# Attention and feed-forward mix on one core: float32 P·V steps in one piece of 512 columns, with a scheduler clock that counts instruction fetches

## The chip, the core and the metric

The kernel runs on one core of a Trainium2 chip. A core has a matrix engine (PE; its weight loads are listed as PEld), a vector engine (DVE), a scalar engine (ACT), a general engine (POOL) and a queue engine that here only starts transfers (SP). Each works through its own list of instructions in order and waits on semaphores for the others. Matmuls write PSUM banks, and the other engines read them from there. The metric is the device time of one execution in microseconds (us).

## The reference

`x` is 2048 x 512. The attention has 32 heads of width 16 with one shared key and value head (`wk`, `wv`: 512 x 16), and no mask; the feed-forward layer has width 1792.

```python
q = (x @ wq).reshape(B, S, H, Dh).transpose(0, 2, 1, 3)
k, v = x @ wk, x @ wv
p = softmax(einsum("bhqd,bkd->bhqk", q, k) * Dh ** -0.5)
a = einsum("bhqk,bkd->bhqd", p, v).transpose(0, 2, 1, 3).reshape(B, S, H * Dh) @ wo
b = einsum("bsf,fd->bsd", silu(einsum("bsd,df->bsf", x, w1)), w2)
g = sigmoid((x * gate_w).sum(-1, keepdims=True))
return g * a + (1 - g) * b
```

## The kernel before

**Stages.** A short first stage (to the first exponential) loads and transposes `x`, makes the keys `KT`, the values `VF` (float32) and `VP` (two halves of 16 columns in 16-bit form), the gate and the first queries. The long stage after it, `attention`, runs the attention and the feed-forward layer together. A second, slower pass over everything stands in the program behind a branch that this input does not take; its instructions are in the program and never run.

**Rounds, steps and scores.** Queries are worked in 32 rounds: 4 chunks of 512 rows x 4 groups of heads x 2 halves. A round has 16 steps, one for each block of 128 keys, so there are 512 steps. A step has two scores (1024 in all). A score (`scores`, L1165) is 8 matmuls of 32 x 512 that fill one of two buffers `S`; then ACT takes the exponential of 128 x 1024 values into half of `P` (L1171). Score number p + 2 reuses the buffer of score p, so it waits for the exponential of p.

**The sums P V** (`sums`, L1260) multiply the step's `P` (128 x 4 x 512) with the values into two accumulators `pv`. There are two ways to do a step:

- *float32* (units "a" and "b"): `P` as it is, with `VF`. Before the change each unit takes 256 of the 512 columns, 8 matmuls in the program, except at the first step of a round, which takes all 512 columns in one piece, again 8 matmuls. The hardware runs one such float32 matmul as two matmuls with two weight loads, so a piece costs 32 PE instructions whether it has 256 or 512 columns.
- *split* (units "U" and "L"): the upper 16 bits of `P` read in place as bfloat16, and the rest, `L`, which DVE makes as a float16 tile by one subtraction of 128 x 2048 (L1190). Each unit is 8 matmuls and 8 weight loads.

Which step goes which way is decided by the scheduler. Even steps are due to be split; an odd step may be split when DVE has time and no other `L` is held (the condition in `scores` with `SPARE`).

**Everything else on PE** is cut into slots of 4 or 8 matmuls: feed-forward layer, output projection and later queries (`Out.product`, L826; `f_slot`). A slot interleaves the tail of one product (rows 64 to 127) with the head of the next (rows 0 to 63). At the end, what remains is done with whole matmuls of 128 columns (`Out.whole`, L830). Products end on DVE (`acc`, L800) or, for the hidden layer, on ACT (tanh into `e`, L840), DVE (L845) and POOL (`H`, L847, L848).

**What sets the order.** The program is written out by a planner in Python. It keeps a clock for PE, ACT, DVE and POOL (`pe[0]`, `act[0]`, ...) with constant costs: a slot of PE takes `SLOT` = 0.2165 us, a U or L unit `VSLOT`, an `L` on DVE `LOW`. In the main loop it works out `due`, the time at which the next score may start (when the exponential two before it has ended), and `room`, the time left until `due + LATER`. It then chooses: sums that fit into `room`, a slot of other work, or the score. `HURRY`, `LASTB`, `NEAR` and `FRESH` say when sums go ahead of slots, and `PB` how many `P` tiles there are. Nothing of this clock is in the program that runs: it only fixes the order on each engine.

Of the kernel before, what the change touches and what calls it, by code (L numbers as in the profile page):

```python
# [25 lines left out]

SLOT, VSLOT, LOW, V_PART = 0.2165, 0.23, 2.37, 1.7
LATER, HURRY, PIECE, PB, FIRST_LOW, LASTB, NEAR, FRESH, SPARE = 0.2, 4, 5.6, 5, 6, 4, 6, 6, 2  # L30

FIRST = "EEEEEEEEEESEESEEEESEEEESBEEEE"
AHEAD, EARLY = 2, (4, 5)
# [14 lines left out]
def kernel(  # L48
# [39 lines left out]
    VF = consts.tile([128, NKT, 32], F32)  # L88
# [648 lines left out]
    def attention(ctx, scale_of, t_scale, shifts, split_pieces, chores, q_todo, bounds, early, gates_, later):  # L737
# [7 lines left out]
        pe, act, dve, pool = [0.0], [0.0], [0.0], [0.0]  # L745
        tasks, L = [], {}

        def put(dur, ready, due, f, hard=False, low=None):

            tasks.append([due, ready, dur, f, hard, low])  # L750
            return tasks[-1]
# [226 lines left out]
        class Turn:  # L978

            cur = new = None  # L980
            i = n = 0
# [59 lines left out]
        def f_slot():  # L1041
            i, cur, new = T_.i, T_.cur, T_.new
            for m in range(4):
                if new and i < new.n:
                    new.product(i, lo, m, i == 0, False)
                if cur and i >= T_.n - cur.n:
                    cur.product(i - T_.n + cur.n, hi_, m, False, i == T_.n - 1)
            pe[0] += SLOT
            if cur and i == T_.n - 1:
                leave(cur)  # L1050
            T_.i += 1
            if T_.i == T_.n:
                T_.cur, T_.new, T_.going, T_.since, T_.chain = new, None, False, scored[0], bool(cur)
# [28 lines left out]
        steps = [(i, kt) for i in range(len(rounds)) for kt in range(NKT)]  # L1082
# [67 lines left out]
        def scores(p):  # L1150
            s, j = divmod(p, 2)
            i, kt = steps[s]
            if p % 2 == 0 and kt == 0:
                prefetch(i + 1)
                if q_todo and i % 2 == 0:
                    queue.append(q_todo.pop(0))
            if j == 0:
                probs[s] = wp.tile([128, 4, 512], F32, name="P", bufs=PB)
            sc = pS.tile([128, 2, 512], F32, name="S")
            pe[0] = max(pe[0], ends.get(p - 2, 0.0) + 0.05)  # L1160
            for m in range(4):
                for f in range(2):
                    b = 64 * f
                    k0 = kt * 128 + 32 * m
                    nc.tensor.matmul(sc[32 * m:32 * m + 32, f], KT[b:b + 50, k0:k0 + 32], qtile[i][b:b + 50, j], start=True, stop=True)  # L1165
            begin = max(act[0], pe[0] + 0.48)
            pe[0] += SLOT
            scored[0] += 1
            P = probs[s]
            c, o, _ = rounds[i]  # L1170
            nc.scalar.activation(P[:, 2 * j:2 * j + 2], sc, AF.Exp, scale=scale_of(c, o))  # L1171
            act[0] = begin + 0.902
            ends[p] = begin + 1.018
            if j and s % 2 == 0:
                if s >= FIRST_LOW or not later:
                    lows[s] = put(LOW, ends[p] + 0.06, ends[p] + 2.66, lambda: low(s), low=lambda: len(L) < 2)
                else:
                    native.add(s)
            elif j and s >= FIRST_LOW:
                lows[s] = put(LOW, ends[p] + 0.06, ends[p] + 40, lambda: low(s), low=lambda: not L and s >= first[0] + SPARE)  # L1180
# [13 lines left out]
        native, units, opened, first, v_end = set(), {}, set(), [0], [1e9 if later else 0.0]  # L1194

        def units_of(s):

            if s in units:
                return units[s]
            return ["U", "L"] if s in low_end or s % 2 == 0 and s not in native else ["a", "b"]  # L1200
# [4 lines left out]
        def can_go(s):  # L1205
            i = steps[s][0]
            if not units_of(s) or ends.get(2 * s + 1, 1e9) + 0.05 > pe[0]:
                return False
            if i and i not in opened and not closed_by(i - 1):
                return False  # L1210
            return units_of(s)[0] in "ab" or max(low_end.get(s, 1e9), v_end[0]) <= pe[0]

        def cost(s):
            return VSLOT if units_of(s)[0] in "UL" else 2 * SLOT if steps[s][0] in opened else 4 * SLOT

        def whole_step(s):
            return lows.get(s) in tasks and units_of(s) == ["U", "L"]

# [7 lines left out]
        def waiting():  # L1226
            s0 = first[0]
            return range(s0, min((s0 // NKT + 1) * NKT, scored[0] // 2))
# [5 lines left out]
        def last_unit(n):  # L1234
            return left_in_round() == 1

        def sums_next(room):
            return next((s for s in waiting() if can_go(s) and cost(s) <= room + (0 if units_of(s)[0] in "UL" else 0.1)), None)

        def sums(s):  # L1240

            i, k = steps[s]
            start = i not in opened
            if start:
                pvs[i] = [pO.tile([128, 512], F32, name=f"pv{h}") for h in range(2)]
                opened.add(i)
            u = units[s] = units_of(s)
            if lows.get(s) in tasks:
                tasks.remove(lows[s])
            rest = sum(len(units.get(q, "ab")) for q in range(i * NKT, i * NKT + NKT))  # L1250
            P = probs[s]
            if u[0] in "UL":
                a, b, cols, n = VP[:, k], upper(P) if u[0] == "U" else L.pop(s), slice(0, 512), 1
            else:
                a, b, n = VF[:, k], P, 2 if start else 1
                cols = slice(0, 512) if start else slice(0, 256) if u[0] == "a" else slice(256, 512)
            pe[0] += cost(s) if not start or u[0] in "UL" else 4 * SLOT
            for j in range(4):
                for h, r in enumerate((lo, hi_)):
                    nc.tensor.matmul(pvs[i][h][32 * j:32 * j + 32, cols], a[r], b[r, j, cols], start=start, stop=rest == n)  # L1260
            del u[:n]
            if not u:
                probs.pop(s)
                while first[0] in units and not units[first[0]]:
                    first[0] += 1
            if rest == n:
                norm_a(i, pvs.pop(i), rounds[i][2], rounds[i][:2])
# [43 lines left out]
        while p < n_s:  # L1311
            serve(pe[0])
            due = ends.get(p - 2, 0.0) + 0.05
            room = due + LATER - pe[0]
            s = first[0]
            behind = p // 2 - s
            if p % 2 == 0 and behind >= PB:
                i = steps[s][0]
                if can_go(s):
                    sums(s)  # L1320
                elif i and i not in opened and not closed_by(i - 1):
                    if closed[i - 1] is None:
                        force(closing[0])
                    pe[0] = max(pe[0], closed[i - 1])
                elif s % 2 == 0 and s not in native and (whole_step(s) or v_end[0] > 1e8):
                    make_native(s)
                else:
                    pe[0] = max(pe[0], low_end.get(s, 0.0), ends[2 * s + 1] + 0.05, v_end[0] if s in low_end else 0.0)
                continue
            if bound_ready() and room >= 0.1:  # L1330
                bound()
                continue
            n = sums_next(room)
            near = left_in_round() <= NEAR
            fresh = T_.going and T_.n - T_.i >= FRESH
            if n is not None and near and not fresh and last_unit(n) and behind < LASTB:
                n = None
            first_sums = behind >= HURRY if not near or behind >= LASTB else fresh or not T_.going
            if n is not None and first_sums:
                sums(n)  # L1340
            elif room >= SLOT and f_ready():
                f_slot()
            elif n is not None:
                sums(n)
            else:
                k = next((k for k in waiting() if k % 2 == 0 and whole_step(k) and ends[2 * k + 1] + 0.05 <= pe[0]
                          and (not k // NKT or k // NKT in opened or closed_by(k // NKT - 1))), None)
                if k is not None and room >= 2 * SLOT:
                    make_native(k)
                elif room >= SLOT and pe[0] + 0.02 < due:  # L1350
                    pe[0] += 0.05
                else:
                    scores(p)
                    p += 1
# [62 lines left out]
```

## Time and profile before

| | |
|---|---|
| median of 3 runs | 1089.44 us (1086.33 to 1089.73) |
| the profiled execution | 1088.11 us, of which 1086.3 us is the span from first to last instruction |
| mean granted TensorE clock | 0.994 |
| PE / ACT / DVE / POOL busy | 1045.3 / 1004.4 / 819.6 / 406.1 us |
| first exponential starts | 40.1 us |
| last exponential starts | 1047.2 us |

All times inside the execution count from the start of the span. Two things help in reading it. Matmuls and exponentials overlap with their successors, so the listed length of one (about 0.38 us and 1.05 us) is longer than the distance between two starts, and a busy share near 100% does not say that the engine could do no more. And instructions reach an engine as blocks that a queue of the transfer engines carries; the profile lists them as a queue of the kind "instruction".

### The profile page before, as it was taken

The page shows a single profiled execution, that of the slowest core. Times are in us where ns is not written, and L with a number is a line of the kernel's source. Part 1 is how long each engine was busy: PE and PEld are TensorE (multiplying, and loading weights), DVE is VectorE, ACT ScalarE, POOL GpSimd, SP SyncE. Part 2 cuts the span into 40 slices and gives each one's busy share as a digit, 9 for nine tenths or more (in the row PEclk, how much of TensorE's full clock was granted, in tenths as well). Part 3 has the DMA queues.
Part 4 walks back from the last instruction along what each step waited for, and adds up shares of the span by engine and source line. Part 5 has one row for each costly group of instructions (what it writes and reads, how often), then busy time and mean ns, then how long its engine had stood idle before and what let it go on. Part 6 is the DMA issues. An engine that isn't in the chain of part 4 may idle for free.

```text
span 1086.3 us, 71852 instructions
## 1 busy us (share of the span) xinstructions
PE 1045.3 (96%) x34030; PEld 646.4 (60%) x34030; DVE 819.6 (75%) x805; ACT 1004.4 (92%) x1121; POOL 406.1 (37%) x388
## 2 busy tenths in 40 slices
PE   7999999999999999999999999999999999999977
PEld 5455556565565666675656565666556666566643
DVE  6798989989898867777677776867768676757673
ACT  5799999999999999999999999999899999999960
POOL 1034428434242354433534334343262126444510
PEclk9999999999999999999999999999999999999998
DMA  5412112100000100000000010000000010000001
GB/s 196 133 51 70 54 41 60 51 12 22 13 18 18 41 21 13 22 12 22 5 22 12 22 51 12 22 6 21 11 12 12 12 42 14 12 12 13 5 4 42
DMA packets 23107, 33.35 MB, mean 31 GB/s; under 512 B 5137, under 2 KB 13074, under 8 KB 22802
## 3 DMA queue, kind: packets, MB, share of 16 engines
q1 hardware_dynamic: 22050, 27.54, 8.1%
q8 instruction: 268, 4.39, 1.7%
q0 software_dynamic: 320, 1.05, 0.3%
q14 instruction: 37, 0.30, 0.1%
q10 hardware_dynamic: 432, 0.07, 0.0%
HBM read 20.12 MB, written 8.52 MB: 26 GB/s over the span
## 4 chain that ended last, share of the span: by engine, by line
PE 76%; DVE 11%; ACT 8%; issue 3%; POOL 1%; DMA 1%; ACTq 0%; DVEq 0%
PE pm L826 27%; PE pv L1260 26%; PE S L1165 18%; ACT P L1171 7%; DVE L L1190 5%; PE pm L830 2%; DVE e L845 1%; DMA gwr<-in_gate_w_dram 1%; DVE w2s L198 0%; DVE w2s L197 0%; ACT e L840 0%; PE pt L316 0%; DVE T L1094 0%; PE pk L128 0%; DVE xs L119 0%
## 5 line engine op out<-in xcount | busy, mean ns | idle before, releaser
L1171 ACT ACTIVATE P<-S 128x1024 f32<-128x1024 f32 x1024 | 962.8, 1066 | 28.9 <-PE S L1165 22.3
L1190 DVE TENSOR_TENSOR L<-P 128x2048 f16<-128x2048 f32 x212 | 505.9, 2389 | 90.7 <-ACT P L1171 90.2
L1165 PE MATMUL S<-qb,KT 50*32 50x512 f16 x8192 | 513.3, 380 | 6.7 <-ACT P L1171 2.7
L1260 PE MATMUL pv<-P,VF 64*32 64x256 f32 (+1 forms) x9392 | 388.5, 381 | 4.3 <-issue 3.7
L1165 PEld LDWEIGHTS <-KT 50*32 50x32 f16 x8192 | 205.6, 90 | 163.6 <-issue 82.6
L826 PE MATMUL pm<-xs,w1s 64*32 64x512 f16 x5376 | 286.9, 376 | 3.8 <-issue 2.0
L826 PE MATMUL pm<-w2s,H 64*32 64x512 f16 x4800 | 284.4, 377 | 1.8 <-issue 0.7
L1260 PEld LDWEIGHTS pv<-P,VF 64*32 64x32 f32 x9392 | 204.3, 106 | 68.9 <-issue 12.6
L1100 POOL TENSOR_TENSOR T<-T,U 128x512 f32<-128x512 f32 x31 | 85.1, 2745 | 285.0 <-DVE U L1095 285.0
L826 PEld LDWEIGHTS <-w1s 64*32 64x32 f16 x5376 | 129.9, 93 | 60.0 <-issue 14.6
L826 PEld LDWEIGHTS <-H 64*32 64x32 f16 x4800 | 128.9, 93 | 44.2 <-issue 11.1
L847 POOL CAST H<-e 128x512 f16<-128x512 f32 x56 | 46.9, 837 | 260.2 <-DVE e L845 258.4
L1260 PE MATMUL pv<-P,VP 64*32 64x512 bf16 x1688 | 111.2, 389 | 1.3 <-issue 0.9
L1260 PE MATMUL pv<-L,VP 64*32 64x512 f16 x1688 | 106.7, 375 | 4.0 <-DVE L L1190 2.4
L848 POOL TENSOR_TENSOR H<-e,H 128x512 f16<-128x512 f32 x56 | 103.4, 1847 | 4.5
L826 PE MATMUL pm<-xs,wqs 64*32 64x512 f16 x1152 | 92.9, 375 | 0.1
L1260 PEld LDWEIGHTS <-VP 64*32 64x32 f16 x3376 | 70.4, 92 | 31.4 <-issue 10.3
L845 DVE SCALAR_TENSOR_TENSOR e<-e,pm 128x512 f32<-128x512 f32 x56 | 38.4, 686 | 51.8 <-ACT e L840 51.3
L826 PE MATMUL pm<-wo_s,O 64*32 64x512 f16 x1440 | 72.3, 375 | 0.3 <-issue 0.3
L800 DVE SCALAR_TENSOR_TENSOR acc<-pm,g,acc 128x512 f32<-128x512 f32 x48 | 35.9, 748 | 31.6 <-PE pm L826 21.7
L1107 POOL TENSOR_TENSOR U<-U 128x48 f32<-128x48 f32 (+1 forms) x62 | 47.3, 763 | 2.4
L826 PEld LDWEIGHTS <-wqs 64*32 64x32 f16 x1152 | 38.6, 92 | 10.7 <-issue 1.6
(175 smaller groups left out, 599.9 us busy)
## 6 DMA issues: line engine op xcount, KB each, us to landing
qb<-qd SPq DMA_DIRECT2D x192, 32.0 KB
raw<-in_B_w_dram SPq DMA_DIRECT2D x22, 256.0 KB
xn<-in_A_x_dram SPq DMA_DIRECT2D x8, 512.0 KB
out_dram<-acc SPq DMA_DIRECT2D x16, 256.0 KB
qd<-qx SPq DMA_DIRECT2D x12, 256.0 KB
raw<-in_B_w_dram POOLq DMA_DIRECT2D x4, 256.0 KB, 3.0
raw<-in_A_wo_dram SPq DMA_DIRECT2D x4, 256.0 KB
qb<-sh SPq DMA_DIRECT2D x62, 2.0 KB
```

What stands on the lines that cost most here:

```text
L800: nc.vector.scalar_tensor_tensor(a, po, gate[:, n:n + 1], a, op0=OP.mult, op1=OP.add)
L826: nc.tensor.matmul(self.bank[32 * m:32 * m + 32], l(i, rows, 32 * m), r(j, rows), start=first, stop=last)
L830: nc.tensor.matmul(self.bank, l(i, slice(0, 128), 0, 128), r(j, slice(0, 128)), start=first, stop=last)
L845: nc.vector.scalar_tensor_tensor(e, e, 1.0, ph, op0=OP.add, op1=OP.mult)
L847: nc.gpsimd.tensor_copy(H[:, 0], e)
L848: nc.gpsimd.tensor_tensor(H[:, 1], e, H[:, 0], op=OP.subtract)
L1100: eng.tensor_tensor(T, T, U, op=OP.add)
L1107: eng.tensor_tensor(first, first, second, op=OP.add)
L1165: nc.tensor.matmul(sc[32 * m:32 * m + 32, f], KT[b:b + 50, k0:k0 + 32], qtile[i][b:b + 50, j], start=True, stop=True)
L1171: nc.scalar.activation(P[:, 2 * j:2 * j + 2], sc, AF.Exp, scale=scale_of(c, o))
L1190: nc.vector.tensor_tensor(L[s], P, upper(P), op=OP.subtract)
L1260: nc.tensor.matmul(pvs[i][h][32 * j:32 * j + 32, cols], a[r], b[r, j, cols], start=start, stop=rest == n)
```

## The change

In the float32 way, every step may now take all 512 columns in one piece, not only the first of a round. `in_one` allows it where both units are still to do and where a piece of four slots ends at most `ONE_LATE` = 0.3 us after `room`; for the first step of a round it is the rule as before. If the one piece doesn't fit, a half of 256 columns may still be taken, but now only when the sums are behind by `HURRY` steps, or when there is no other slot to run.

The planner's clock for PE now counts the instructions that it writes (`issue`): 16 for a score, a slot, a U or an L, 32 for a float32 piece of either size. When the count passes a multiple of 256, the clock may not be less than `BLOCK` = 3.65 us after the previous such point.

`SPARE` goes from 2 to 0, so an odd step may be split from DVE as soon as no `L` is held, if it has not been summed; `NEAR` goes from 6 to 4 and `FRESH` from 6 to 8. No engine gets a new kind of instruction.

```diff
-SLOT, VSLOT, LOW, V_PART = 0.2165, 0.23, 2.37, 1.7
-LATER, HURRY, PIECE, PB, FIRST_LOW, LASTB, NEAR, FRESH, SPARE = 0.2, 4, 5.6, 5, 6, 4, 6, 6, 2
+SLOT, VSLOT, LOW, V_PART, BLOCK, ONE_LATE = 0.2165, 0.23, 2.37, 1.7, 3.65, 0.3
+LATER, HURRY, PIECE, PB, FIRST_LOW, LASTB, NEAR, FRESH, SPARE = 0.2, 4, 5.6, 5, 6, 4, 4, 8, 0
...
+        sent, crossed = [0], [-9.0]
+
+        def issue(n, dur):
+
+            if sent[0] // 256 != (sent[0] + n) // 256:
+                pe[0] = crossed[0] = max(pe[0], crossed[0] + BLOCK)
+            sent[0] += n
+            pe[0] += dur
...
-            pe[0] += SLOT
+            issue(16, SLOT)
...
-            begin = max(act[0], pe[0] + 0.48)
-            pe[0] += SLOT
+            issue(16, SLOT)
+            begin = max(act[0], pe[0] + 0.48 - SLOT)
...
+        def in_one(s, room):
+            return len(units_of(s)) == 2 and (steps[s][0] not in opened or 4 * SLOT <= room + ONE_LATE)
...
-        def sums_next(room):
-            return next((s for s in waiting() if can_go(s) and cost(s) <= room + (0 if units_of(s)[0] in "UL" else 0.1)), None)
+        def sums_next(room, halves=True):
+
+            def fits(s):
+                if not halves and len(units_of(s)) == 2 and units_of(s)[0] == "a":
+                    return in_one(s, room)
+                return cost(s) <= room + (0 if units_of(s)[0] in "UL" else 0.1)
+
+            return next((s for s in waiting() if can_go(s) and fits(s)), None)
...
-            start = i not in opened
+            start, one = i not in opened, in_one(s, room)
...
-                a, b, n = VF[:, k], P, 2 if start else 1
-                cols = slice(0, 512) if start else slice(0, 256) if u[0] == "a" else slice(256, 512)
-            pe[0] += cost(s) if not start or u[0] in "UL" else 4 * SLOT
+                a, b, n = VF[:, k], P, 1 + one
+                cols = slice(0, 512) if n == 2 else slice(0, 256) if u[0] == "a" else slice(256, 512)
+            issue(16 if u[0] in "UL" else 32, VSLOT if u[0] in "UL" else 2 * n * SLOT)
...
-            n = sums_next(room)
+            n = sums_next(room, False)
...
+            if n is None and behind >= HURRY:
+                n = sums_next(room)
...
-                sums(n)
+                sums(n, room)
...
-            elif n is not None:
-                sums(n)
+            elif n is not None or sums_next(room) is not None and not (near and not fresh and last_unit(0) and behind < LASTB):
+                sums(n if n is not None else sums_next(room), room)
```

What the planner makes of it shows only in the order of the program that it writes. One place on PE, in the chunk of scores around number 300 of 1024, before: the last matmul of a score, the first half of a float32 step (`P_10108`), a slot of other work, the next score, and the second half of the same step. `S` is the score's buffer, `pv0` and `pv1` the accumulators, and the last number is the columns of a matmul.

```order
L1165 MATMUL S_10353<-qb1_82,KT_60 32x512
L1260 MATMUL pv0_10007<-P_10108,VF_62 32x256
L1260 MATMUL pv1_10008<-P_10108,VF_62 32x256
...
L826 LDWEIGHTS O_7208
L826 MATMUL pm_10283<-wo_s_69,O_7208 32x512
...
L1165 LDWEIGHTS KT_60
L1165 MATMUL S_10380<-qb1_82,KT_60 32x512
L1260 MATMUL pv0_10007<-P_10108,VF_62 32x256
L1260 MATMUL pv1_10008<-P_10108,VF_62 32x256
```

PE near the same score in the changed program: a score, one float32 piece of 512 columns of one step (`P_9590`), and at once the next score.

```order
L1174 MATMUL S_9754<-qb1_82,KT_60 32x512
L1278 MATMUL pv0_9653<-P_9590,VF_62 32x512
L1278 MATMUL pv1_9654<-P_9590,VF_62 32x512
...
L1174 LDWEIGHTS KT_60
L1174 MATMUL S_9775<-qb1_82,KT_60 32x512
```

The step that stood on both sides of a score is now one block of 8 matmuls between two scores, and takes half as many instructions.

The other place is DVE late in the run, steps 434 to 442 of 512, before. Each `L` row is one split step; the four `P` are those of steps 434, 436, 440 and 442; the rows between them end hidden-layer products (`e`) and a round (`rr`, `C`).

```order
L1190 TENSOR_TENSOR L_29137<-P_29006 128x2048
L845 SCALAR_TENSOR_TENSOR e_29165<-e_29165,pm_28752 128x512
L1190 TENSOR_TENSOR L_29278<-P_29167 128x2048
L1115 RECIPROCAL rr_29365<-T_29004 128x16
L1118 TENSOR_TENSOR C_29367<-T_29004,rr_29365 128x16x16
L845 SCALAR_TENSOR_TENSOR e_29396<-e_29396,pm_28987 128x512
L1190 TENSOR_TENSOR L_29549<-P_29444 128x2048
L845 SCALAR_TENSOR_TENSOR e_29612<-e_29612,pm_29243 128x512
L1190 TENSOR_TENSOR L_29687<-P_29585 128x2048
```

DVE over the same steps in the changed program; the `P` are those of steps 434, 437, 438, 440, 443 and 444.

```order
L1199 TENSOR_TENSOR L_27999<-P_27842 128x2048
L854 SCALAR_TENSOR_TENSOR e_28051<-e_28051,pm_27637 128x512
L1199 TENSOR_TENSOR L_28154<-P_28061 128x2048
L1199 TENSOR_TENSOR L_28251<-P_28118 128x2048
L854 SCALAR_TENSOR_TENSOR e_28261<-e_28261,pm_27872 128x512
L1124 RECIPROCAL rr_28339<-T_27861 128x16
L1127 TENSOR_TENSOR C_28341<-T_27861,rr_28339 128x16x16
L1199 TENSOR_TENSOR L_28378<-P_28263 128x2048
L854 SCALAR_TENSOR_TENSOR e_28473<-e_28473,pm_28129 128x512
L1199 TENSOR_TENSOR L_28568<-P_28475 128x2048
L1199 TENSOR_TENSOR L_28657<-P_28532 128x2048
```

Two odd steps (437 and 443) are split as well, and DVE has two `L` in a row in two places.

Counted over the part of the program that runs, by the order:

| on PE, in the long stage | before | after |
|---|---|---|
| float32 pieces of 512 columns | 15 | 201 |
| float32 pieces of 256 columns | 572 | 134 |
| split steps (U and L), and of them odd steps | 211, 0 | 244, 34 |
| PE instructions (a float32 piece as 32) | 67,732 | 60,892 |
| whole matmuls at the end (`Out.whole` with `H`) | 72 | 60 |

More of the change, by code (lines that the diff above doesn't have):

```diff
@@ L1235, in last_unit, with sums @@
             return left_in_round() == 1
-        def sums_next(room):
-            return next((s for s in waiting() if can_go(s) and cost(s) <= room + (0 if units_of(s)[0] in "UL" else 0.1)), None)
-        def sums(s):
+        def sums_next(room, halves=True):
[4 more added lines that the diff above has]
+            return next((s for s in waiting() if can_go(s) and fits(s)), None)
+        def sums(s, room=9.0):
             i, k = steps[s]
-            start = i not in opened
+            start, one = i not in opened, in_one(s, room)
             if start:
```

## The prediction

> **What bounds the kernel now.** I read the page first, for busy times and queues, then the exponentials, because their number is fixed.
>
> ```profile
> PE 1045.3 (96%) x34030; PEld 646.4 (60%) x34030; DVE 819.6 (75%) x805; ACT 1004.4 (92%) x1121; POOL 406.1 (37%) x388
> q8 instruction: 268, 4.39, 1.7%
> ```
>
> PE and ACT both look full, so busy shares cannot tell which one leads. How fast exponentials can follow each other is told by three in a row, and by one behind a tanh (view: order of time on ACT):
>
> ```profile
> L1171 ACT ACTIVATE P<-S x1024: 1016/1045/1236, 40.1 to 1047.2; 128x1024 f32<-128x1024 f32 x171
> 1045.42 2.85 ACT L1171 ACTIVATE P<-S 128x1024 f32<-128x1024 f32 x3
> 805.06 0.60 ACT L840 ACTIVATE e<-pm 128x512 f32<-128x512 f32 x1
> 805.54 2.88 ACT L1171 ACTIVATE P<-S 128x1024 f32<-128x1024 f32 x3
> L840 ACT ACTIVATE e<-pm x56: 589/618/771, 62.8 to 1053.4; 128x512 f32<-128x512 f32 x56
> ```
>
> Three take 2.85 us and one about 1.045, so starts are (2.85 - 1.045) / 2 = 0.904 us apart at best; a tanh delays the next by 0.48 us, and 54 of the 56 lie before the last exponential. The floor of the stretch from first to last exponential is 1023 x 0.904 + 54 x 0.48 = 950.7 us. It takes 1047.2 - 40.1 = 1007.1 us, so 56.4 us are lost to waiting. That is all that a faster PE can win there.
>
> What ACT waits for is the score from PE. PE itself shows pauses that no semaphore explains, best seen on its weight loads (view of waits, whole run, all loads that waited for "issue" in the long stage; then four of them in order of time, then the transfer queues from 515 to 527 us):
>
> ```profile
> PEld L1165 <- issue: 82.6, 327, 1.3
> PEld L826 <- issue: 29.0, 64, 1.5
> PEld pv L1260 <- issue: 12.6, 22, 2.9
> PEld L1260 <- issue: 10.3, 17, 1.4
> ```
>
> ```profile
> 517.48 0.09 PEld L1165 LDWEIGHTS <-KT 50*32 50x32 f16 x1 [0.17 <-issue]
> 518.12 0.11 PEld L1165 LDWEIGHTS <-KT 50*32 50x32 f16 x6 [0.55 <-issue]
> 522.14 0.34 PEld L826 LDWEIGHTS <-w1s 64*32 64x32 f16 x22 [0.66 <-issue]
> 525.89 0.11 PEld L826 LDWEIGHTS <-w1s 64*32 64x32 f16 x6 [0.41 <-issue]
> ```
>
> ```profile
> q8 instruction: 3, 0.05, 1.5%
> ```
>
> The 0.17 before a score is ordinary. The other three come 4.02 and 3.75 us apart, one for each of three blocks of instructions. The page's 268 blocks for 2 x 34,030 matmuls and loads make 254 instructions a block. A block holds 16 slots, and a slot of 16 instructions lasts about 0.216 us (804.31 to 804.53 in a fence below), so its work is 3.46 us: PE asks for blocks slightly faster than they come, and stops in mid-slot. In PE's rows of the timeline I count 76 gaps between matmul starts (75.24 to 1044.41, over 0.30 us each) that end 2.0 to 3.1 us after such a block's transfer began and 1.1 to 1.75 us after it landed (gaps that belong to the pattern of float32 matmuls left out). They lose 37.7 us, less the usual spacing; 66 of them, with 31.6 us, have no semaphore at their end.
>
> Two neighbouring stretches show what this does to ACT (views: exponentials alone, then all of ACT, then the waits of the loads in either):
>
> ```profile
> 546.00:590.00 44.00, 41.54 (x44) 1.00 0.06 17
> 590.00:649.00 59.00, 58.49 (x65) 1.00 0.11 34
> 546.00:590.00 44.00, 41.92 (x45) 1.00 0.06 17
> 590.00:649.00 59.00, 59.00 (x67) 1.00 0.11 34
> PEld L826 <- issue: 1.5, 4, 0.6
> PEld pv L1260 <- issue: 1.4, 2, 0.8
> PEld L1260 <- issue: 1.4, 2, 0.8
> ...
> PEld L1260 <- issue: 0.3, 1, 0.3
> PEld L826 <- issue: 0.3, 1, 0.3
> ```
>
> With 8 such waits outside the scores, 44 exponentials and one tanh, worth 40.3 us, take 44. With two, 65 and two tanh, worth 59.7, take 59.0: ACT at its floor. So the stretch from 546 is bound by the arrival of instructions, the next by ACT.
>
> **The change, part by part.** Counts are those of the order; durations are from the profiled execution.
>
> *Float32 steps in one piece.* Pieces fall from 587 to 335, 252 x 32 = 8,064 instructions. Split steps add 33 x 32 = 1,056, and 84 matmuls for slots 168. In all 6,840 of 67,732 go, 26.7 blocks. The array's work of a piece of 512 columns is the same as two halves:
>
> ```profile
> 804.31 0.41 PE L1165 MATMUL S<-qb,KT 50*32 50x512 f16 x8
> 804.53 1.05 PE L1260 MATMUL pv<-P,VF 64*32 64x512 f32 x16
> 805.39 0.41 PE L1165 MATMUL S<-qb,KT 50*32 50x512 f16 x8
> ```
>
> 0.86 us for 32 instructions, against four slots with 64. A block that holds one lasts 3.46 + 0.43 = 3.89 us and no longer outruns its successor. By the order, 247 of 265 blocks before hold no such step, 74 of 238 now. So I leave 30% of the stalls. Of a stall, 0.83 reached ACT: in 115 windows of 8 scores after the 96th, the 61 without a stall lost 0.155 us over the floor, the 54 with 0.70 us of stall lost 0.73. Low end of the saving: 37.7 x 0.70 x 0.83 = 22 us. High end: all loss after the first 96 scores (56.4 - 6.7) behaves as the two stretches above, x 0.70 = 35 us. I take the middle, **29 us**, since the second stretch speaks for the high end and the counted gaps for the low one.
>
> *The same piece delays the next score.* In the rows above the scores are 1.08 us apart, yet at 805.54 ACT runs three without a wait; so one piece is hidden by the second score buffer. But intervals between scores with six or more slots of PE work rise from 35 to 93. In the 32 of them behind score 96, exponentials came 0.12 us late on average; for the 58 new ones, with longer intervals among them, I take 0.15 each, **8.7 us** (0 if all hide; 186 x 0.43 = 80 if each new piece pushes its score by its second half).
>
> *33 more split steps.* Each replaces four slots by two on PE, 33 x 0.43 = 14 us, off the path where ACT leads: nothing. On DVE they add 33 x 2.389 = 79 us:
>
> ```profile
> L1190 DVE TENSOR_TENSOR L<-P 128x2048 f16<-128x2048 f32 x212 | 505.9, 2389 | 90.7 <-ACT P L1171 90.2
> 100.00:400.00 300.00, 292.41 (x9975) 177.65 (x9967) 266.07 (x239) 293.11 (x324) 125.26 (x108) 1.00 0.12 34
> 400.00:700.00 300.00, 294.54 (x10159) 186.13 (x10151) 214.56 (x170) 292.32 (x321) 120.41 (x105) 1.00 0.07 19
> PE pv L1260 <- DVE L L1190: 2.4, 3, 1.0
> ```
>
> DVE (third busy figure) is 89% busy from 100 to 400 us and 72% after. The order puts 29 of the 33 behind score 320 of 1024, where 79 us in some 690 make it 83%. Queued behind an `L` on DVE are the evictions that free PE's banks. PE waited for an `L` three times, 2.4 us. I take **1 us** (nothing to 33 x 1.0, the longest such wait).
>
> *The clock, `NEAR`, `FRESH` and `SPARE`* issue nothing; what they do is in the counts above. POOL, ACT and SP have as many rows as before, and PE's list is the same up to the first scores, so the 40.1 us ahead stay.
>
> *The end.* (order of time on PE)
>
> ```profile
> 1049.62 0.57 PE L1260 MATMUL pv<-L,VP 64*32 64x512 f16 x8
> 1058.61 5.30 PE L830 MATMUL pm<-wo_s,O 128*128 128x512 f16 x12 [5.30 <-DVE O L1126]
> 1063.71 15.77 PE L830 MATMUL pm<-w2s,H 128*128 128x512 f16 x72
> ```
>
> From the last exponential to the end are 39.1 us, a chain through the last round's division on DVE, then whole matmuls. Of the 72 only 60 are left: 12 x 15.77 / 72 = **-2.6 us**. Both programs end their sums with the `L` of step 510, so the chain starts alike.
>
> Sum: 40.1 + 950.7 + (56.4 - 29 + 8.7 + 1) + (39.1 - 2.6) = 1064.4 us of span. The profiled execution is 1.8 us longer than its span (1088.1 against 1086.3): **1066 us**. It is 1.3 below the median of the runs, which I let stand.
>
> **Rivals.**
> - *Late scores win back the loss (slower).* The planner lets a piece end 0.3 us later than anything else. If each of the 186 new pieces made ACT wait, the price of one decides: above (29 + 2.6 - 1) / 186 = 0.16 us the gain is gone; at 0.25 us it is 46.5 for 8.7, 1104 us. The row at 804.53 speaks against it; but that piece had short intervals around it, and now some intervals have eight slots. Chance 0.10.
> - *The pauses aren't the blocks' (slower).* Then fewer instructions save nothing: 1088.1 + 8.7 + 1 - 2.6 = 1095 us. Pauses once per block speak against it. Chance 0.05. The Trainium skill says as much in "Runtime: NRT & Kernel Launch", Instruction fetch mechanics: crossing a block boundary is "one DMA tail-bump, mostly hidden"; by that rule the sum would be that of this rival, and the rows at 518.12, 522.14 and 525.89 disagree with it.
> - *DVE becomes the bound.* An `L` ahead of an eviction stops slots and then scores. At 1.0 us for each of the 33, 1066 + 32 = 1098; at half, 1082. The 89% in the first third speaks for it, the place of the new ones against it. Chance 0.07 for the former.
> - *Stalls vanish altogether.* If blocks on average 3.46 x 265 / 238 = 3.85 us long (and longer at ACT's pace) let the array catch up, all 49.7 us go and the pieces hide: 1088.1 - 49.7 - 2.6 + 1 = 1037 us; half of the way from the forecast, 1051. Chance 0.15 below 1050.
>
> **How the numbers follow.** The forecast has 0.63, with its own range 1050 to 1083: the saving from 22 to 35 and the late scores from 0 to about twice 8.7. With the rivals' ends, the range that leaves about 0.1 on either side is 1046 to 1091. A difference of 0.3% (3.3 us) is about what can be told from none. Faster: 0.63 + 0.15, and 0.02 of rivals that stop short, 0.80. Same: 0.05, from rivals whose price comes out near 0.16 us. Slower: 0.15.
>
> **What would show it.** Right: instruction blocks near 241 instead of 268; waits for "issue" of loads outside the scores well below 52 us; exponentials from first to last in about 987 us; `L` x245 on DVE with few PE waits for it. Wrong: ACT waits for scores right behind pieces of 512 columns, pauses that stay at one per block, or PE waits for `L`, for `e` or for `acc` that weren't there.

## The result and the profile after

The changed kernel takes 1075.41 us (median of 4 runs, 1072.54 to 1079.13) against 1088.81 us for the kernel before in the same comparison: a ratio of 0.9882, 95% interval 0.9842 to 0.9923. The forecast was 1066, range 1046 to 1091: a gain of some 22 us, of which 13 came. The profiled execution took 1073.23 us (span 1071.4), 14.9 us less than that of before.

First the page of the changed kernel (busy times, the `L` of DVE, the queue that brings instructions), then the exponentials alone:

```profile
PE 1023.1 (95%) x30610; PEld 564.2 (53%) x30610; DVE 916.6 (86%) x838; ACT 999.7 (93%) x1121; POOL 471.2 (44%) x388
q8 instruction: 241, 3.95, 1.6%
L1199 DVE TENSOR_TENSOR L<-P 128x2048 f16<-128x2048 f32 x245 | 606.8, 2491 | 35.8 <-ACT P L1180 35.2
```

```profile
L1180 ACT ACTIVATE P<-S x1024: 1015/1068/1278, 39.3 to 1037.6; 128x1024 f32<-128x1024 f32 x171
```

Blocks of instructions fell from 268 to 241, as counted from the order. First to last exponential is 1037.6 - 39.3 = 998.3 us against 1007.1: only 8.8 us of the gain. The end, from the last exponential, is 33.8 us against 39.1: 5.3 us. The start gave 0.8.

The floor of the exponentials is still 951 us, so 47 us are lost there. I put each lateness of an exponential (over 0.904 us after an exponential, 0.48 after a tanh) to what PE did since the score before: a gap that no semaphore ends, a gap that a semaphore ends, or no gap, only much work. Sorted a second time by the same rule, single rows came out up to about 2 us different, so no row is better than that.

| lateness of exponentials, us | before | after |
|---|---|---|
| behind PE gaps without a semaphore | 27.2 | 4.5 |
| behind PE gaps that end with a semaphore | 7.4 | 14.4 |
| behind PE work without a gap | 18.0 | 24.6 |
| each under 0.03 | 2.9 | 2.3 |

Of the 66 pauses without a semaphore that end after a block's transfer (31.6 us) one is left (0.4 us). What took their place is work, and waiting for DVE.

The row of work hides two movements. Sorted by the order, the loss behind long intervals between scores (six or more slots, the score among them) rose from 3.1 us in 34 of them to 16.4 in 92; behind shorter ones it fell from 17.1 to 8.2.

Waits of PE for ACT and for DVE before (the view of waits; those for an `L` stand ahead of the result):

```profile
PE S L1165 <- ACT P L1171: 2.7, 5, 1.0
PE pm L826 <- DVE e L845: 1.2, 2, 1.0
...
PE pm L378 <- DVE e L935: 0.4, 1, 0.4
...
PE pm L826 <- DVE acc L800: 0.2, 1, 0.2
```

Waits of PE in the changed kernel (the view of waits, those from 2.4 us on that lie in the long stage):

```profile
PE S L1174 <- ACT P L1180: 11.0, 30, 1.0
PE pm L835 <- DVE e L854: 5.1, 7, 1.0
...
PE pm L378 <- DVE e L944: 3.3, 5, 1.2
PE pv L1278 <- DVE L L1199: 2.8, 7, 0.8
PE pm L835 <- DVE acc L809: 2.4, 3, 1.4
```

The first row is new in size (2.7 us before): PE now often stands ready before ACT has freed the buffer. The rest are slots and L units behind DVE: for `e` and `acc` PE waits 13.4 us in all, where it was 1.8.

One view misled the prediction's own test. Waits of weight loads for "issue" did not fall:

```profile
PEld L1174 <- issue: 161.1, 590, 1.3
PEld L835 <- issue: 33.5, 78, 1.8
PEld L1278 <- issue: 20.9, 61, 1.2
```

Outside the scores there were 52 us before, and there are 66 now (with two small groups). Loads beside a matmul that waits for DVE are put down to "issue" too: of this idle time some 37 us now stand beside such waits for `e`, `acc`, `L` and the like, and 12 before. Without them it fell, from about 40 us to about 27. Gaps between matmul starts that follow a transfer are the better measure.

The end, in order of time on PE:

```profile
1039.87 0.52 PE L1278 MATMUL pv<-L,VP 64*32 64x512 f16 x8
1040.52 2.77 PE L835 MATMUL pm<-w2s,H 64*32 64x512 f16 x48
1046.83 4.63 PE L839 MATMUL pm<-wo_s,O 128*128 128x512 f16 x12 [3.54 <-DVE O L1135]
1051.57 13.11 PE L839 MATMUL pm<-w2s,H 128*128 128x512 f16 x60
```

The 60 whole matmuls take 13.11 us for 15.77, as forecast. The output projection also starts 9.2 us behind the last exponential instead of 11.4.

### The profile page after: what moved, and what is told of

It reads as the page before. It is cut to its first block, busy times and chain, and to the rows that moved or that the text cites. A ratio compares the mean times of both kernels' runs of the same rounds, so it can differ in the third digit from the quotient of the medians.

```text
span 1071.4 us, 65086 instructions
## 1 busy us (share of the span) xinstructions
PE 1023.1 (95%) x30610; PEld 564.2 (53%) x30610; DVE 916.6 (86%) x838; ACT 999.7 (93%) x1121; POOL 471.2 (44%) x388
## 4 chain that ended last, share of the span: by engine, by line
PE 38%; ACT 35%; DVE 13%; issue 8%; POOL 4%; DMA 1%; ACTq 0%; SPq 0%; DVEq 0%; POOLq 0%
ACT P L1180 33%; PE pm L835 13%; PE pv L1278 12%; PE S L1174 9%; DVE L L1199 7%; PE pm L839 2%; ACT e L849 2%; POOL T L1109 1%; POOL U L1111 1%; DVE e L854 1%; PE pt L316 1%; DVE acc L809 1%; POOL T L1112 1%; POOL H L856 0%; POOL U L1116 0%
## 5 line engine op out<-in xcount | busy, mean ns | idle before, releaser
L1180 ACT ACTIVATE P<-S 128x1024 f32<-128x1024 f32 x1024 | 959.6, 1079 | 24.4 <-PE S L1174 22.7
L1199 DVE TENSOR_TENSOR L<-P 128x2048 f16<-128x2048 f32 x245 | 606.8, 2491 | 35.8 <-ACT P L1180 35.2
L1174 PE MATMUL S<-qb,KT 50*32 50x512 f16 x8192 | 435.0, 380 | 13.5 <-ACT P L1180 11.0
L1174 PEld LDWEIGHTS <-KT 50*32 50x32 f16 x8192 | 191.6, 89 | 244.5 <-issue 161.1
L1278 PE MATMUL pv<-P,VF 64*32 64x512 f32 (+1 forms) x5360 | 298.2, 503 | 0.0
L835 PE MATMUL pm<-xs,w1s 64*32 64x512 f16 x5376 | 263.7, 375 | 2.3 <-DVE e L854 1.1
L835 PE MATMUL pm<-w2s,H 64*32 64x512 f16 x4896 | 249.2, 375 | 4.9 <-DVE acc L807 2.0
L835 PEld LDWEIGHTS <-w1s 64*32 64x32 f16 x5376 | 116.1, 92 | 53.3 <-issue 14.9
L835 PEld LDWEIGHTS <-H 64*32 64x32 f16 x4896 | 106.2, 92 | 46.5 <-issue 6.3
L1278 PEld LDWEIGHTS pv<-P,VF 64*32 64x32 f32 x5360 | 104.7, 106 | 37.4 <-issue 6.6
L1111 POOL TENSOR_TENSOR U<-T,mu 128x96 f32<-128x96 f32 x31 | 45.5, 1468 | 2.4
```

Source lines behind the costliest of these rows:

```text
L835: nc.tensor.matmul(self.bank[32 * m:32 * m + 32], l(i, rows, 32 * m), r(j, rows), start=first, stop=last)
L1111: eng.tensor_tensor(z[:, :, 1:1 + DIGITS], T3[:, :, 17:17 + DIGITS], mu[:, :, 1:].to_broadcast([128, 16, DIGITS]), op=OP.mult)
L1199: nc.vector.tensor_tensor(L[s], P, upper(P), op=OP.subtract)
```

## The experiments

Two theories stood at the start: that fewer instruction blocks end the pauses and so make the gain; and that the gain comes from the new order, the split odd steps and the shorter end. Later ones ask which part of the change costs what. Line numbers are those of each kernel; ratios are to the kernel before.

**e1 and e2: the blocks alone.** The order of the changed program stays; one piece is issued as two halves in its place. In `sums`, for e1:

```diff
-            for j in range(4):
-                for h, r in enumerate((lo, hi_)):
-                    nc.tensor.matmul(pvs[i][h][32 * j:32 * j + 32, cols], a[r], b[r, j, cols], start=start, stop=rest == n)
+            apart = n == 2 and not start and True
+            for part in (slice(0, 256), slice(256, 512)) if apart else (cols,):
+                for j in range(4):
+                    for h, r in enumerate((lo, hi_)):
+                        nc.tensor.matmul(pvs[i][h][32 * j:32 * j + 32, part], a[r], b[r, j, part], start=start, stop=rest == n and part.stop == cols.stop)
```

e2 has `s // 2 % 2` for `True`.

> The changed program with its order kept, but each of the 185 float32 pieces of 512 columns that don't open a round is issued as two pieces of 256 columns back to back: the same work of the array in the same place, 5,920 PE instructions more (66,812 against 60,892, 261 blocks against 238). Theory (the gain is the end of the pauses at instruction blocks): the pauses return, some 30 us of them between matmul starts where the changed program has almost none without a semaphore, and the time rises by 15 to 30 us, to 1090 to 1105. Rival (the gain comes from the new order, the split odd steps and the shorter end, not from fewer instructions): 1075, within 3 us.

> The same with every second pair of steps: 97 of the 185 pieces in halves, 3,104 instructions more (250 blocks). Theory: between the two, about half of the rise, 1082 to 1092. Rival: 1075, within 3 us.

e1 took 1086.09 us, ratio 1.0005 (0.9973 to 1.0037); e2 1073.91 us, ratio 0.9891 (0.9812 to 0.9969). With all halves, no gain over the kernel before can be told, in the same order and with the same split steps and the same end (33.9 and 33.8 us after the last exponential). Where nothing interrupts them, two halves take 0.864 us and one piece 0.860, so the 185 pieces account for under 1 us by themselves. The exponentials and the blocks, first of e1, then of e2:

```profile
q8 instruction: 264, 4.33, 1.7%
L1180 ACT ACTIVATE P<-S x1024: 1014/1044/1276, 39.3 to 1049.9; 128x1024 f32<-128x1024 f32 x171
```

```profile
q8 instruction: 253, 4.15, 1.7%
L1180 ACT ACTIVATE P<-S x1024: 1016/1067/1278, 39.1 to 1038.2; 128x1024 f32<-128x1024 f32 x171
```

In e1 the stretch is 12.2 us longer, and 27 pauses without a semaphore are back (13.2 us). Two of them in order of time, on the weight loads of e1, in slots of other work:

```profile
546.55 0.11 PEld L835 LDWEIGHTS <-H 64*32 64x32 f16 x8 [0.61 <-issue]
550.57 0.09 PEld L835 LDWEIGHTS <-wqs 64*32 64x32 f16 x1 [0.79 <-issue]
```

They are 4.02 us apart, as in the kernel before. The second theory falls as the cause of the gain. But e1 came out below the range of the first (1090 to 1105), e2 inside the range of its rival (1075, within 3), and the cost isn't in proportion: the first 3,104 instructions cost nothing, the next 2,816 some 12 us. In the long stage a block lasts 999.1 / 250 = 4.00 us in e2 and 1010.5 / 261 = 3.87 in e1 (before: 1007.1 / 264.6 = 3.81). These times hold the pauses themselves. Between these two the transfers stop being hidden in this order. Counted the same way over the long stretch, e6 and e7 below fall in line: at 3.92 us a block e6 has 23 such pauses (11.5 us), at 4.05 e7 has 4 (1.8 us). The Trainium skill calls crossing a block "mostly hidden" (Runtime: NRT & Kernel Launch, Instruction fetch mechanics); e2 agrees, e1 and the kernel before show where it ends.

**e3: half the work of each `L`.** The other half of the correction is left out.

```diff
-            nc.vector.tensor_tensor(L[s], P, upper(P), op=OP.subtract)
+            nc.vector.tensor_tensor(L[s][:, 0:2], P[:, 0:2], upper(P)[:, 0:2], op=OP.subtract)
...
-                    nc.tensor.matmul(pvs[i][h][32 * j:32 * j + 32, cols], a[r], b[r, j, cols], start=start, stop=rest == n)
+                    nc.tensor.matmul(pvs[i][h][32 * j:32 * j + 32, cols], a[r], b[r, j % 2 if u[0] == "L" else j, cols], start=start, stop=rest == n)
```

> The changed program with its order kept, but DVE makes only half of each L (128 x 1024 of 128 x 2048), and the matmuls of the L unit read that half twice, so the correction of the other half is left out. DVE is relieved of about 245 x 1.2 = 290 us. Theory (what is left between the exponentials is partly slots and L units that wait for DVE, 15 us by their semaphores): the time falls by 8 to 15 us, to 1060 to 1067. Rival (late scores behind long intervals of PE work make up what is left): 1073 to 1076.

1061.81 us, ratio 0.978 (0.9699 to 0.986), 13.6 us below the changed kernel. The page and the exponentials:

```profile
PE 1023.0 (96%) x30610; PEld 562.5 (53%) x30610; DVE 643.8 (61%) x838; ACT 996.7 (94%) x1121; POOL 338.7 (32%) x388
L1180 ACT ACTIVATE P<-S x1024: 1016/1090/1279, 39.1 to 1027.1; 128x1024 f32<-128x1024 f32 x171
```

First to last exponential is 10.4 us shorter; lateness behind semaphores goes from 14.4 to 1.4 us. So DVE does hold up some 10 us in the changed kernel. But 36.8 us over the floor stay lost with DVE at 61%, so DVE isn't all of the rest. POOL's busy time fell by 132 us though its work is the same.

**e4: no odd steps split.** In the line of constants, `SPARE` 0 becomes 999.

> The changed planner with SPARE at 999, so that no odd step is split: 214 split steps against 244, 225 float32 pieces of 512 columns against 201, about the same number of instructions (61,084). DVE loses 30 L, 75 us; PE gains 30 x 0.43 = 13 us of array work and 24 more long pieces. Theory (DVE's load costs about 7 us more than before the change, PE has room): 1070 to 1076, not slower. Rival (the odd splits pay by keeping PE short): 1080 to 1088.

1072.43 us, ratio 0.9875 (0.9795 to 0.9954): not to be told from the changed kernel. Lateness behind semaphores is 7.5 us for 14.4, that behind work 31.1 for 24.6. Here taking out the odd splits moves the loss and doesn't remove it: PE then has the work that DVE had.

**e5 to e8: one part alone, one part away.** The line of constants in each (`BLOCK, ONE_LATE` and `NEAR, FRESH, SPARE`; the changed kernel has 3.65, 0.3 and 4, 8, 0):

```diff
 e5 one piece alone:  BLOCK, ONE_LATE = 0.0, 0.3     NEAR, FRESH, SPARE = 6, 6, 2
 e6 clock alone:      BLOCK, ONE_LATE = 3.65, -9.0   NEAR, FRESH, SPARE = 6, 6, 2
 e7 no lateness:      BLOCK, ONE_LATE = 3.65, 0.0    NEAR, FRESH, SPARE = 4, 8, 0
 e8 no clock:         BLOCK, ONE_LATE = 0.0, 0.3     NEAR, FRESH, SPARE = 4, 8, 0
```

> The one piece alone: the changed planner with a clock that counts no blocks (BLOCK 0) and NEAR, FRESH, SPARE as before (6, 6, 2). 239 pieces of 512 columns and 136 of 256, 205 split steps, none of them odd; 61,428 PE instructions (240 blocks), and only 24 whole matmuls of H left for the end against 60. Theory (fewer instructions end the pauses, whatever the clock): no pauses without a semaphore, first to last exponential near the 998 us of the changed kernel, an end 36 x 0.22 = 8 us shorter, 1064 to 1072. Rival (the counting clock, by pacing PE, is what helps): 1080 to 1090.

> The clock alone: counted blocks (BLOCK 3.65), ONE_LATE at -9 so that only the first step of a round goes in one piece, NEAR, FRESH, SPARE as before. 12 pieces of 512 and 554 of 256 columns, 65,596 instructions (256 blocks), 120 whole matmuls at the end against 72 before. Theory: 256 blocks lie between the 250 that cost nothing and the 261 that cost 12 us, so pauses of 10 to 20 us stay, and the end is 48 x 0.22 = 10 us longer than before: 1086 to 1096. Rival (the clock is what helps): 1070 to 1080.

> The changed planner with ONE_LATE at 0: 90 pieces of 512 and 362 of 256 columns, 241 split steps, 63,028 instructions (246 blocks), intervals of six slots or more between scores 51 instead of 93, 120 whole matmuls at the end instead of 60. Theory (long intervals cost about 7 us more than before the change): first to last exponential 4 to 8 us shorter than the 998 us, the end 13 us longer: 1078 to 1086. Rival (late scores cost nothing): first to last exponential as before, 1085 to 1090.

> The changed planner with BLOCK at 0 and all else kept: 211 pieces of 512 and 130 of 256 columns, 236 split steps, 61,416 instructions (240 blocks), 93 long intervals, 18 whole matmuls at the end instead of 60. Theory (the clock only moves slots from between the scores to the end): first to last exponential within 6 us of 998, the end 9 us shorter, 1064 to 1074. Rival (a planner that doesn't count blocks overfills PE): first to last exponential above 1010 us, 1078 to 1090.

| | median us | ratio (95%) | first to last exponential | last exponential to end |
|---|---|---|---|---|
| changed | 1075.41 | 0.9882 (0.9842 to 0.9923) | 998.3 | 33.8 |
| e5 | 1062.93 | 0.9771 (0.9713 to 0.9828) | 996.0 | 26.0 |
| e6 | 1099.89 | 1.0113 (1.0079 to 1.0147) | 994.4 | 66.0 |
| e7 | 1095.05 | 1.0063 (1.0040 to 1.0086) | 995.3 | 58.9 |
| e8 | 1076.41 | 0.9884 (0.9828 to 0.9941) | 1008.7 | 24.7 |

The one piece alone is worth 25 us, about twice the whole change. The counting clock alone costs 11.5 us. It makes the planner think PE slower, so fewer slots go between the scores and more are left for the end. In e6 the stretch is 12.7 us shorter than before the change and the end 27 longer; 6 more tanh lie behind the last exponential, 6 x 0.48 = 2.9 of the 12.7. The pauses that its theory expected stayed, 11.5 us of them. The expectation of e6 counted only the whole matmuls of `H`; the end has others as well (by shape, on PE):

```profile
L839 PE MATMUL pm<-w2s,H 128*128 128x512 f16 x120 | 26.2, 379 | 0.0
L839 PE MATMUL pm<-xs,w1s 128*128 128x512 f16 x84 | 18.5, 379 | 0.2 <-DVE acc L809 0.2
```

Its time fits neither theory's range; that the clock alone helps is refuted, and so is my size of the end. e7 missed the same way: the stretch is 3.0 us shorter than in the changed kernel, and the end 25 longer, not 13. Of the 3.0, 5 tanh that moved to the end are 2.4, so fewer long intervals (51 for 93) won almost nothing: the loss behind them fell by 5.6 us, and that behind shorter ones rose by 5.1. In e8 the end came as expected, but the stretch is 1008.7 us, in neither range; lateness behind semaphores is 19.3 us. e5 and e8 differ only by `NEAR`, `FRESH` and `SPARE`, which e9 and e10 take apart.

**e9 to e12: from e5, one constant at a time.**

```diff
 e9:   e5 with NEAR, FRESH, SPARE = 6, 6, 0
 e10:  e5 with NEAR, FRESH, SPARE = 4, 8, 2
 e11:  e5 with ONE_LATE = 0.45
 e12:  e5 with ONE_LATE = 0.22
```

> The kernel with the one piece alone (e5, 1063 us) with SPARE at 0 instead of 2, nothing else: 232 split steps against 205, 220 pieces of 512 columns against 239, 239 blocks, 24 whole matmuls at the end as in e5, long intervals 80 against 89. Theory (the odd splits load DVE, and PE then waits behind slots and L units): losses of ACT behind semaphores rise from 3.5 us by 8 to 14, 1069 to 1077. Rival (NEAR and FRESH made the difference between e5 and e8): 1063, within 4.

> e5 with NEAR 4 and FRESH 8, nothing else: 207 split steps, 230 pieces of 512 columns, 240 blocks, 36 whole matmuls at the end against 24 (2.6 us). Theory (odd splits make the difference): 1062 to 1069. Rival (NEAR and FRESH): 1072 to 1078.

> e5 with ONE_LATE at 0.45: 288 pieces of 512 columns against 239, 42 of 256 against 136, 235 blocks, 169 long intervals against 89, none of the whole matmuls of H left at the end (24 x 0.22 = 5 us less). Theory (a long interval costs about 0.12 us): first to last exponential 8 to 12 us longer, the end 5 shorter, 1064 to 1071. Rival (long intervals are hidden): 1055 to 1060.

> e5 with ONE_LATE at 0.22: 203 pieces of 512 columns, 210 of 256, 243 blocks, 69 long intervals against 89, 48 whole matmuls at the end against 24. Theory: the exponentials gain 2 to 3 us, the end loses 5, 1063 to 1068. Rival (blocks count even here): above 1070.

| | median us | ratio (95%) | first to last exponential | last exponential to end |
|---|---|---|---|---|
| e9 | 1071.68 | 0.9848 (0.9814 to 0.9882) | 1005.7 | 24.8 |
| e10 | 1062.37 | 0.9763 (0.9727 to 0.9799) | 992.1 | 28.7 |
| e11 | 1067.51 | 0.9803 (0.9768 to 0.9838) | 1006.2 | 19.6 |
| e12 | 1065.87 | 0.9797 (0.9762 to 0.9832) | 993.8 | 31.0 |

Odd splits cost 8.8 us where no clock holds PE back; `NEAR` and `FRESH` alone nothing. Both together (e8) cost 13.5, and no run takes the 5 us beyond the two apart. The `L` of DVE and PE's longest waits for them, first e5, then e9:

```profile
L1199 DVE TENSOR_TENSOR L<-P 128x2048 f16<-128x2048 f32 x206 | 493.9, 2401 | 81.4 <-ACT P L1180 80.9
PE pm L835 <- DVE e L854: 4.4, 9, 0.7
PE pv L1278 <- DVE L L1199: 0.2, 1, 0.2
```

```profile
L1199 DVE TENSOR_TENSOR L<-P 128x2048 f16<-128x2048 f32 x233 | 576.1, 2486 | 35.9 <-ACT P L1180 35.5
PE pv L1278 <- DVE L L1199: 7.2, 15, 1.2
PE pm L835 <- DVE e L854: 3.7, 5, 1.1
```

27 odd steps more make PE wait 7.2 us for an `L` where it waited 0.2. e10 and e4 split no odd step and differ in the clock alone: 1062.37 and 1072.43, with intervals that just touch, 5.4 us in the stretch and 6.0 at the end. e11 and e12 show `ONE_LATE` weighing the stretch against the end: later pieces fill PE better and leave 19.6 us at the end, but the exponentials take 10.2 us more than in e5; earlier ones the reverse.

So from e5's -25 us the clock gives back about 10, and odd splits beside the clock 3 that can't be told from none. The parts don't add up, and this is one order of taking them: with odd splits in, the clock costs nothing in the time (e8 without it 1076.41, the changed kernel 1075.41), because what it adds at the end (9 us) it saves in the stretch (10). e5 and e10 beat both kernels; between these two the runs don't decide.

## Why the prediction was right or wrong

**The bound and the mechanism: right.** Pauses once per block of instructions bound the kernel before, and the one piece ended them: 268 blocks became 241 and the pauses without a semaphore one. e1 shows the cause: with the blocks put back into the same order no gain can be told. Two signs that the prediction gave came (241 blocks, few waits for an `L`); the exponentials took 998 us, not 987, and the waits for `e` and `acc` that it listed as a sign of being wrong are there.

**"I take the middle, 29 us": about right, if delays passed on are counted.** Lateness right behind such gaps fell from 27.2 to 4.5 us, 22.7, the low end of the term (22). Behind short intervals of plain work it fell by another 8.9, and e1, which brings the pauses back, has 6 of these again (14.2 for 8.2), so a part of that was pauses handed on to later scores. How much, no run says: the saving lies between 23 and 32 us.

**"So I leave 30% of the stalls": wrong.** One pause of 66 is left. That the low end of 22 us, which holds the factor 0.70, fits the 22.7 is luck. A share that falls in proportion to blocks doesn't hold; e2 has pauses almost gone at 250 blocks. What goes with it is the time of a block: at 4.00 us the pauses are hidden, at 3.87 not.

**"8.7 us" for late scores: too low.** The 58 new long intervals brought 13.3 us of lateness behind work, 0.23 us each for the 0.15 taken. As a net price it can be smaller, since fewer long intervals put work elsewhere: e11, with 80 more of them than e5, lost 10.2 us in the stretch, 0.13 us each, and e7, with 42 fewer than the changed kernel, won almost nothing.

**"I take 1 us" for 33 more split steps: the term that was furthest off.** Lateness behind semaphores rose by 7.0 us, and e3, with DVE relieved, gives back 10.4. The prediction counted the waits for an `L` alone, and took each at 2.389 us. DVE's busy time rose by 97 us, not 79: an `L` took 2.491 on average, since it met POOL more often and lost more where it did. The same 56 casts of `H` and 62 small additions on POOL, before and after:

```profile
L1107 POOL TENSOR_TENSOR U<-U 128x48 f32<-128x48 f32 (+1 forms) x62 | 47.3, 763 | 2.4
L847 POOL CAST H<-e 128x512 f16<-128x512 f32 x56 | 46.9, 837 | 260.2 <-DVE e L845 258.4 <-DVE raw L678 1.8
```

```profile
L856 POOL CAST H<-e 128x512 f16<-128x512 f32 x56 | 57.7, 1030 | 205.9 <-DVE e L854 204.3
L1116 POOL TENSOR_TENSOR U<-U 128x48 f32<-128x48 f32 (+1 forms) x62 | 57.4, 925 | 2.4
```

Most of the added wait isn't for `L` at all, but for `e` and `acc` queued behind one, which the prediction named and then priced at nothing. The other half of the step, that the relief of PE is worth nothing, was off as well: without the odd splits (e4) lateness behind semaphores falls by 6.9 us, that behind work rises by 6.5, and the time is the same. So in this kernel the odd splits cost and saved about as much; only in e9 do they cost 8.8.

**The clock, "issue nothing; what they do is in the counts above": incomplete.** The counts in the prediction had no row for the slots that the clock leaves to the end, beside the 72 and 60 whole matmuls. Where no odd step is split it costs about 10 us (e4 against e10, 60 and 36 of them); where they are, nothing (e8). Seen from the kernel before, the end still became shorter, by 5.3 for the 2.6 forecast, since the last round's products reached PE earlier as well.

**Rivals.** DVE as the bound had the right engine and at most a fifth of its price. Late scores didn't win back the loss, at 13 us for 8.7. That the pauses were not the blocks' is refuted by e1. That all stalls vanish came true, without the time that it gave: the pieces weren't hidden.

Term by term against 1066, with the shorter intervals counted to the stalls: these are as forecast within 3 us, DVE adds 6 and late scores 5, and the end takes off 3 and the start 1, about the 7 us between 1066 and the profiled 1073.2; the medians add 2. That the time is only 9 us off is in part luck, since two costs and two savings were all put too low.

## What to carry to other kernels

Count the instructions of a busy PE against the time they have: here, in one order, blocks of 256 that last 4.0 us cost nothing, and at 3.87 us they cost 12. So wide float32 matmuls pay by being fewer; their work is the same. When an engine is relieved, look at what else the same change loads: a second engine's long operation, queued ahead of short ones that others wait for, here added 7 us of waiting, a third of what the pauses had cost right behind them. And a planner's clock that counts one more limit of the chip can still give a worse order, if it leaves work for the end that would have fitted between; try each part alone, and with the others, since here the prices of the parts don't add up.

## What the runs showed of the hardware that was not expected

- One or two transfers of an instruction block, between 750 and 775 us, took 2.7 to 4.9 us in the kernels whose transfers I listed one by one (before, changed, e1 to e4), against a median of 1.1 us and at most 2.0 for the others; why stays open. In the kernel before and in e4 PE then stood still for 2.8 us, in e3 for 3.4, and after it the granted clock was half; in the changed kernel PE did not stand still. The kernel before, its windows ahead of the pause, in it, behind it, and after:

```profile
764.00:767.20 3.20, 2.97 (x96) 1.91 (x95) 2.55 (x2) 2.56 (x4) 0.00 (x0) 1.00 0.23 39
767.20:770.10 2.90, 0.45 (x20) 0.00 (x1) 0.22 (x1) 0.47 (x1) 0.00 (x0) 1.00 0.04 6
770.30:773.70 3.40, 3.40 (x72) 2.52 (x68) 1.59 (x3) 2.05 (x2) 1.47 (x2) 0.50 0.11 29
773.70:777.00 3.30, 3.30 (x123) 2.37 (x115) 2.77 (x2) 3.03 (x4) 3.22 (x4) 1.00 0.02 5
```

The column after POOL is the clock: 0.50 for 3.4 us. In e4 a pause of 2.8 us was followed by 6.8 us at 0.50. The Trainium skill asks for no idle gaps of PE over about 3 us (TensorE: Matmul & The Clock Gate, Why this matters for your kernels); here 2.8 us was enough twice. But the changed kernel had 3.4 us at 0.50 after a pause of 1.7 us, and e8 kept 1.00 after one of 3.0, so these runs show no length at which it happens.

- DVE and POOL slow each other. Before, the 116 `L` that met no work of POOL took 2.288 us, the 84 that met it for more than 2 us 2.451, and 10 that met 0.5 to 1.2 us of it 3.04. After, the groups are 98, 116 and 26 with 2.286, 2.511 and 3.17. With DVE relieved in e3, POOL's busy time for the same work is 338.7 us instead of 471.2.
